# Eight float32 products of zeros ahead of TensorE's first work, in a chunked scan followed by two feed-forward layers

## The chip, the cores and the metric

One Trainium2 chip, one of its cores. The metric is the device time of one execution, in microseconds (us); lower is better. The kernel was timed in three runs; a fourth execution was recorded by the hardware profiler, and all rows below are from that one.

## The reference

Three stages, one after the other; everything is float32.

```python
# 1. chunked decayed scan, batch 4, heads 8, sequence 768, head dim 32, state 16
L = exp(cum[i] - cum[j]) * causal           # cum: running sum of log(clip(a))
y = (C B^T * L) x  +  (C state) * exp(cum)  # inside a chunk, plus the carried state
state = decay * state + sum_j B_j x_j * decay_from_j
# 2. first layer: 3072 tokens, 256 -> 2048 -> 256
h = x @ w_in;  x = where(h > 0, h, exp(min(h, 0)) - 1) @ w_out
# 3. second layer: 256 -> 1536 -> 256
g = x @ w_gate;  out = (g * sigmoid(g) * (x @ w_val)) @ w_out
```

## The kernel before, in words

The 3072 tokens are cut into 24 units of 128 tokens (unit t is chunk t // 4 of batch t % 4) and into six blocks of 512. The first layer runs block by block over 16 slices f of its width (two groups of products per slice: `h` into PSUM, L558, then `c`, L599 in block 0 and L607 in the later blocks); the second layer runs over 36 steps after it. The scan of a block's four units must be done before the block's first `h` can start. For blocks 1 to 5 that work is laid between the slices of the block before; for block 0 there is nothing in front of it, so units 0 to 3 form a prologue of about 22 us.

The order of work on each engine is the order in which the program issues it (a manual schedule; each engine takes its instructions in order). In the prologue that order is written out by hand in the string `ORDER` (L65): each word stands for one step. The words that matter here, with their lines:

- `La0`, `ca0` (L323, L329, L331): loads the decays of unit 0 as an 8-row table and clips them. `ba0` (L337) spreads that table over 128 partitions with two float32 products of 256 columns; the result is read by `E0`. `bp0`, `bp1` (L341) do the same for the running products, read by `P0`, `P1` (L355).
- `cl1` (L360, L364) clips the decays of unit 1, which came by DMA. `E0` (L350) and `E1` to `E3` (L370) are scans on VectorE over the decays. `el` (L413, ScalarE) and `bn` (L407, GpSimd) scale B with the result.
- `cb0` to `cb3` (L437): 16 small products C B^T per unit, even units into the PSUM tile `cb`, odd units into `cb_odd` (named cbo in the trace, two banks). `m0` to `m3` (L443) multiply E with them.
- `u` (L454), `sc` (L465), `sn` (L477), `y` (L524, L514), `out` (L542, ScalarE), `xl` (L546, VectorE): the unit's state, its output, and the output split into a high part `xh` and a low part `xl`, which are the operands of `h`. Units 1 and 3 share the PSUM tile yo for their outputs.
- `d00`, `d10`, `d20` and so on (L139, L142, L146, VectorE), `ex` (L136, ScalarE), `wh` (L184, ScalarE), `wl` (L190, GpSimd): decoding of float64 weights into a high and a low float32r part, `wih` and `wil`. Batch 0 (`d.0`) gives the first layer's weights of slices 0 and 1, batch 1 those of 2 and 3, batch 2 the `wov` of c in slices 0 and 1.

In block 0 a slice f goes: `m_a` (six products h, L558, into one of two PSUM buffers), `m_e1` (ScalarE, L580), `m_e1b` (ScalarE, L585, then VectorE, L586, which reads h a last time and so frees its buffer), and, two slices later, `m_c` (two float32 products c, L599). The weight decoding of the later slices is laid on VectorE between these steps.

A float32 product stands in the trace as two matmul records and two weight loads; a float32r product (L558, L607) as one of each. `zero_q` (L812) is a tile of 128x128 zeros that VectorE sets first of all; in the kernel before it is an operand of the running products at L386 alone.

Of the kernel before, what the change touches and what calls it, by code (L numbers as in the profile page):

```python
# [18 lines left out]
Q = 128  # L19
# [47 lines left out]
def ssm_mlp_glu_kernel(ctx, tc, a, bcs, xbc, w1, w2, consts, out):  # L67
    nc = tc.nc
# [10 lines left out]
    zero_q = const.tile([128, Q], F32, name="zero_q")  # L79
# [26 lines left out]
    cb_odd = first.enter_context(tc.tile_pool(name="ps0", bufs=1, space=PSUM)).tile([128, 2, 512], F32, name="cbo")  # L106
# [46 lines left out]
    def load_w1(j):  # L153
        if j >= 4:
            raw = w2e[:, j % 5 * 1024:(j % 5 + 1) * 1024]
        else:
            raw = {2: w2e[:, 1024:2048], 3: w2e[:, 5120:]}.get(j)
        kind, p = batches[j]
        w1s[j] = [None, *decode(w1.bitcast(U32)[kind == "o", p], raw)]
        w1s[j][1]()  # L160

    def ex_w1(j):
        w1s[j][2]()

    def dec_w1(j, steps=(0, 1, 2)):
        kind, p = batches[j]
        if w1s[j][0] is None:
            if kind == "i":
                w1s[j][0] = stg.tile([128, 512], F32, tag="v", name="v", bufs=VB)
            else:  # L170
                w1s[j][0] = W1["ov", p] = w1p.tile([128, 512], F32, tag="wo", name="wov", bufs=NF1 // 2)
                for i, z in enumerate(halves):
                    W1["v", 2 * p + i] = w1s[j][0][:, z]
        for k in steps:
            w1s[j][3][k](w1s[j][0])
# [5 lines left out]
    def hi_w1(j):  # L181
        kind, p = batches[j]
        if kind == "i":
            nc.scalar.activation(W1["ip", p][0], w1s[j][0], AF.Copy)  # L184

    def lo_w1(j):
        kind, p = batches[j]
        v = w1s.pop(j)[0]
        if kind == "i":
            nc.gpsimd.tensor_tensor(W1["ip", p][1], v, W1["ip", p][0].bitcast(F32), ALU.subtract)  # L190
# [620 lines left out]
    with tc.manual_schedule():  # L811
# [24 lines left out]
        for f in range(6):  # L836
            tok[f"LW{f}"] = lambda f=f: load_w1(f)
            tok[f"ex{f}"] = lambda f=f: ex_w1(f)
            for k in range(3):
                tok[f"d{k}{f}"] = lambda f=f, k=k: dec_w1(f, (k,))  # L840
            tok[f"wh{f}"] = lambda f=f: hi_w1(f)
            tok[f"wl{f}"] = lambda f=f: lo_w1(f)
        for z in ORDER:
            tok[z]()
        first.close()
# [190 lines left out]
```

## Time and profile before

| what | value |
|---|---|
| three runs | 607.23, 607.78, 607.55 us; median 607.55 |
| the profiled execution | 607.43 us |
| its span, first to last instruction | 605.6 us |
| mean granted TensorE clock | 0.998 |
| busy share | PE 98%, DVE 74%, POOL 58%, ACT 58% |

PE is TensorE's matmuls, PEld its weight loads, DVE is VectorE, ACT is ScalarE, POOL is GpSimd. The time of an execution is its span and 1.8 us around it. Matmul records overlap: the end of one is modelled and lies after the start of the next, so the rate of TensorE is read from the distance between starts, and a busy share near 100% need not be full speed. The last three columns of such a row name the operation, its tiles and their shapes; square brackets give the idle time of the engine just before, and what ended it.

### The profile page before, as it was taken

The page shows a single profiled execution, that of the slowest core. Times are in us where ns is not written, and L with a number is a line of the kernel's source. Part 1 is how long each engine was busy: PE and PEld are TensorE (multiplying, and loading weights), DVE is VectorE, ACT ScalarE, POOL GpSimd, SP SyncE. Part 2 cuts the span into 40 slices and gives each one's busy share as a digit, 9 for nine tenths or more (in the row PEclk, how much of TensorE's full clock was granted, in tenths as well). Part 3 has the DMA queues.
Part 4 walks back from the last instruction along what each step waited for, and adds up shares of the span by engine and source line. Part 5 has one row for each costly group of instructions (what it writes and reads, how often), then busy time and mean ns, then how long its engine had stood idle before and what let it go on. Part 6 is the DMA issues. An engine that isn't in the chain of part 4 may idle for free.

```text
span 605.6 us, 9763 instructions
## 1 busy us (share of the span) xinstructions
PE 593.6 (98%) x3524; PEld 469.5 (78%) x3524; DVE 450.6 (74%) x684; ACT 350.0 (58%) x623; POOL 352.4 (58%) x318
## 2 busy tenths in 40 slices
PE   5999999999999999999999999999999999999997
PEld 4656667887888888878888788887888888888785
DVE  6898867777888879985765688878766777766665
ACT  1565657776668766776976555554434444433333
POOL 3543559998888877874685667754333334333331
PEclk9999999999999999999999999999999999999999
DMA  7698533346666446732000111100100000100001
GB/s 205 251 287 239 181 99 99 129 124 172 200 200 187 176 183 202 228 127 80 27 27 26 53 53 53 52 1 1 70 1 0 1 1 1 69 1 0 2 0 69
DMA packets 22743, 58.69 MB, mean 97 GB/s; under 512 B 3736, under 2 KB 6168, under 8 KB 22696
## 3 DMA queue, kind: packets, MB, share of 16 engines
q1 hardware_dynamic: 20664, 53.18, 28.5%
q10 hardware_dynamic: 2032, 4.90, 2.1%
q8 instruction: 27, 0.44, 0.3%
q14 instruction: 20, 0.16, 0.1%
HBM read 50.12 MB, written 7.96 MB: 96 GB/s over the span
## 4 chain that ended last, share of the span: by engine, by line
PE 85%; DVE 4%; ACT 1%; issue 1%; DMA 0%; POOL 0%; SPq 0%; DVEq 0%
PE h L558 18%; PE c L607 17%; PE o L722 16%; PE pc L746 8%; PE pd L746 8%; PE pa L746 8%; PE pb L746 4%; PE cb L432 2%; PE y L509 2%; PE c L599 1%; PE y L505 1%; DVE E L370 1%; DVE m L586 0%; DVE wov L139 0%; DVE wov L142 0%
## 5 line engine op out<-in xcount | busy, mean ns | idle before, releaser
L755 POOL TENSOR_TENSOR gl<-m,gh 128x512 fp32r<-128x512 f32 x70 | 94.1, 1346 | 136.0 <-ACT gh L753 136.0
L564 POOL TENSOR_TENSOR gl<-m,gh 128x512 fp32r<-128x512 f32 x80 | 111.7, 1397 | 39.1 <-ACT gh L563 37.4
L586 DVE SCALAR_TENSOR_TENSOR m<-m,h 128x512 f32<-128x512 f32 x96 | 65.6, 683 | 50.0 <-ACT m L585 49.4
L580 ACT ACTIVATE m<-h 128x512 f32<-128x512 f32 x96 | 56.9, 593 | 48.7 <-PE h L558 43.6
L558 PE MATMUL h<-xh,wih 128*128 128x512 f32 x192 | 80.9, 423 | 0.9 <-ACT xh L542 0.6
L558 PE MATMUL h<-xh,wil 128*128 128x512 f32 x192 | 75.5, 395 | 0.0
L766 DVE TENSOR_TENSOR ident<-s,pb 128x512 f32<-128x512 f32 x36 | 24.8, 688 | 50.8 <-PE pb L746 40.2
L607 PE MATMUL c<-gh,woh 128*128 128x512 f32 x160 | 62.4, 390 | 0.0
L607 PE MATMUL c<-gh,wol 128*128 128x512 f32 x160 | 62.3, 389 | 0.0
L585 ACT ACTIVATE m<-m 128x512 f32<-128x512 f32 x96 | 59.9, 624 | 0.5
L558 PE MATMUL h<-xl,wih 128*128 128x512 f32 x192 | 60.1, 395 | 0.0
L722 PE MATMUL o<-gh,w2h 128*128 128x512 f32 x144 | 56.1, 389 | 0.0
L722 PE MATMUL o<-gh,w2l 128*128 128x512 f32 x144 | 56.0, 389 | 0.0
L722 PE MATMUL o<-gl,w2h 128*128 128x512 f32 x144 | 55.9, 389 | 0.0
L563 ACT ACTIVATE gh<-m 128x512 fp32r<-128x512 f32 x80 | 50.1, 626 | 5.9 <-DVE m L586 5.7
L783 ACT ACTIVATE pc<-pc 128x512 f32<-128x512 f32 x36 | 21.0, 582 | 53.4 <-DVE pc L781 53.4
L607 PE MATMUL c<-gl,woh 128*128 128x512 f32 x160 | 50.9, 389 | 0.0
L778 ACT ACTIVATE m<-pa 128x512 f32<-128x512 f32 x36 | 21.5, 598 | 49.4 <-PE pa L746 49.4
L392 POOL TENSOR_TENSOR xb<-xb,P 128x128 f32<-128x128 f32 x16 | 38.0, 2374 | 14.2 <-DVE P L386 14.2
L558 PEld LDWEIGHTS h<-xh,wih 128*128 128x128 f32 x192 | 36.4, 190 | 12.3 <-DVE m L586 1.5
L753 ACT ACTIVATE gh<-m 128x512 fp32r<-128x512 f32 x72 | 45.2, 628 | 0.9 <-DVE m L788 0.2
L762 ACT ACTIVATE s<-pa 128x512 f32<-128x512 f32 x36 | 21.5, 598 | 37.7 <-PE pa L746 37.7
(235 smaller groups left out, 1433.9 us busy)
## 6 DMA issues: line engine op xcount, KB each, us to landing
w2e<-in_w SPq DMA_DIRECT2D x12, 768.0 KB
abc<-ac SPq DMA_DIRECT2D x16, 512.0 KB
bcraw<-in_bcs SPq DMA_DIRECT2D x32, 256.0 KB
w2e<-in_w SPq DMA_DIRECT2D x14, 512.0 KB
xb<-in_xbc SPq DMA_DIRECT2D x18, 256.0 KB
v2d<-w2e ACTq DMA_DIRECT2D x12, 384.0 KB
v<-v2d SPq DMA_DIRECT2D x12, 384.0 KB
out_y<-x SPq DMA_DIRECT2D x12, 256.0 KB
```

The source lines that it names most:

```text
L392: nc.gpsimd.tensor_tensor(u["ct"], u["ct"], u["P"], ALU.mult)
L558: nc.tensor.matmul(dst, lhsT=l, rhs=r, start=first and i == 0, stop=last and i == len(ops) - 1, **kw)
L563: nc.scalar.activation(hi, src, AF.Copy)
L564: lo_eng.tensor_tensor(lo, src, hi.bitcast(F32), ALU.subtract)
L580: nc.scalar.activation(m, h, AF.Relu, scale=-1.0)
L585: nc.scalar.activation(m, m, AF.Exp, scale=-1.0)
L586: nc.vector.scalar_tensor_tensor(m, m, -1.0, h, ALU.add, ALU.max)
L607: nc.tensor.matmul(cps[b][m], lhsT=w[:, m * 128:(m + 1) * 128], rhs=r, start=f == 0 and w is wh and r is gh, stop=f == NF1 - 1 and r is gl)
L722: nc.tensor.matmul(ops_[p, i, m], lhsT=l, rhs=r, start=f == 0 and k == 0, stop=f == NF2 - 1 and k == 2)
L746: nc.tensor.matmul(ps[k], lhsT=l, rhs=r, start=first and i == 0, stop=i == 2, skip_group_check=True)
L753: nc.scalar.activation(hi, m, AF.Copy)
L755: eng.tensor_tensor(lo, m, hi.bitcast(F32), ALU.subtract)
```

## The change

Eight products are issued to TensorE ahead of every step of `ORDER`. Both operands are `zero_q`: 128x128 as the weights, and the same tile read four times over as 512 moving columns. They write the two banks of `cb_odd` in turn, each product as a group of its own. Nothing reads the result; `cb1` writes the same banks later, again with a start of its own.

```diff
@@ -840,6 +840,9 @@
             tok[f"wl{f}"] = lambda f=f: lo_w1(f)
+        for z in range(8):
+            nc.tensor.matmul(cb_odd[:, z % 2].rearrange("p (a q) -> p a q", q=Q), lhsT=zero_q, rhs=zero_q.unsqueeze(1).to_broadcast([128, 4, Q]),
+                             start=True, stop=True)
         for z in ORDER:
             tok[z]()
```

## Rows read from the trace of the kernel before

**Rows 1.** The page: PE's busy tenths and granted clock in 40 slices.

```profile
PE   5999999999999999999999999999999999999997
...
PEclk9999999999999999999999999999999999999999
```

**Rows 2.** Timeline of PE to 30 us: start, length, line, tiles, shape, records.

```profile
3.29 2.07 PE L337 MATMUL y<-w2e 8*128 8x256 f32 x4 [3.29 <-DVE w2e L331]
...
19.95 0.68 PE L524 MATMUL yo<-w2e,x 64*32 64x64 f32 x32
20.56 0.79 PE L514 MATMUL yo<-x,sbd 128*128 128x128 f32 x2
22.00 1.22 PE L558 MATMUL h<-xh,wih 128*128 128x512 f32 x2 [0.64 <-ACT xh L542]
23.02 1.05 PE L558 MATMUL h<-xl,wih 128*128 128x512 f32 x2
...
26.43 0.83 PE L558 MATMUL h<-xh,wil 128*128 128x512 f32 x2
27.19 0.69 PE L437 MATMUL cb<-bcraw 16*64 16x64 f32 x32
27.81 0.50 PE L558 MATMUL h<-xh,wih 128*128 128x512 f32 x1
```

**Rows 3.** Chain of work that ended last: start, length, what, number of records.

```profile
75.12 1.72 PE c L599 x4
...
95.77 1.36 PE h L558 x6
```

**Rows 4.** Line L599: durations in ns (min/median/max), first and last start, shape.

```profile
L599 PE MATMUL c<-m,wov x64: 590/592/593, 29.3 to 86.3; 128*128 128x512 f32 x64
```

**Rows 5.** Line L524: durations of one shape before and after 26 us.

```profile
L524 PE MATMUL y<-E,x x96: 216/216/241, 49.9 to 73.0; 64*32 64x64 f32 x96
...
L524 PE MATMUL yo<-E,w2e x32: 307/310/311, 17.1 to 17.7; 64*32 64x64 f32 x32
```

**Rows 6.** Timeline of DVE to 50 us.

```profile
0.83 0.17 DVE L812 MEMSET zero_q<- 128x128 f32 x1 [0.83 <-PEq L1027]
...
6.16 0.43 DVE L360 TENSOR_SCALAR abc<-abc 128x512 f32<-128x512 f32 x1 [2.73 <-DMA abc<-in_a]
...
6.70 1.27 DVE L350 TENSOR_TENSOR_SCAN E<-y,x 128x256 f32<-128x256 f32 x2
7.89 1.20 DVE L370 TENSOR_TENSOR_SCAN E<-abc,x 128x512 f32<-128x512 f32 x1
...
21.98 0.42 DVE L546 TENSOR_TENSOR xl<-yo,xh 128x256 fp32r<-128x256 f32 x1 [0.37 <-ACT xh L542]
...
26.25 0.69 DVE L586 SCALAR_TENSOR_TENSOR m<-m,h 128x512 f32<-128x512 f32 x1 [0.44 <-ACT m L585]
```

**Rows 7.** Waits of DVE, 6.7 to 26.9 us: us in total, times, longest.

```profile
DVE wov L146 <- ACT e L136: 0.6, 1, 0.6
DVE m L586 <- ACT m L585: 0.4, 1, 0.4
DVE xl L546 <- ACT xh L542: 0.4, 1, 0.4
DVE x L465 <- PE cbo L454: 0.3, 1, 0.3
DVE w2e L355 <- PE cb L341: 0.2, 1, 0.2
DVE w2e L443 <- ACT x L413: 0.2, 1, 0.2
```

**Rows 8.** Waits of PE, from 26.86 us to the end.

```profile
PE cb L432 <- DVE zc L319: 0.4, 1, 0.4
PE h L558 <- DVE m L586: 0.2, 1, 0.2
```

**Rows 9.** Waits of DVE, 24 to 90 us.

```profile
DVE x L477 <- POOL sbd L481: 4.4, 4, 1.4
```

## The prediction

> **What bounds the kernel now.** I read the page first, then TensorE's timeline, then VectorE's timeline and its waits. On the page PE is busy in every slice of the span but the first, where it is at five tenths [rows 1]: after the prologue the kernel is a queue of matmuls, and from 26.86 us to the end PE waits 0.6 us in all [rows 8]. So whatever moves the first block's products moves the end, unless something between takes it up.
>
> The prologue is the other way round. From `E0` at 6.70 us to `m0`'s last step at 26.25 [rows 6] VectorE waits six times, for 2.1 us in 20 [rows 7]; the rest is its own in-order work. PE, ScalarE and GpSimd serve it. So the question is when that run on VectorE starts, and which of its six waits go away.
>
> TensorE's clock is the third thing to see. The granted clock reads full in all 40 slices [rows 1], but the distances between starts say otherwise. Between the starts at 23.02 and 26.43 us lie eight products of 512 columns, so 0.43 us each [rows 2]; later six of the same shape take 1.36 us, 0.23 each [rows 3]. [...] The small products of line 524 show the same, 310 ns at 17 us and 216 ns from 49 us on [rows 5]. So the whole prologue ran at the low level, though PE had something in hand for much of it, and the clock rose only near 26.8 us, 4.8 us after the dense products began at 22.00.
>
> **The change part by part.**
>
> *The eight products.* A float32 product is two records; the four records of `c` in one slice take 1.72 us at the high level, 0.43 each [rows 3]. Sixteen records are 16 x 0.43 = 6.9 us at the high level and 13.8 at the low one. They wait only for `zero_q`, which VectorE has set at 0.83 + 0.17 = 1.0 us [rows 6], so I let them start at 1.05. The unknown is T, how long they run at the low level. The nearest row is the one rise in this trace, 4.8 us after dense work began. The end is then 1.05 + 6.9 + T/2 = 10.3 us. The bounds: 7.9 if the clock were high from the first record, 14.8 if it never rises under zeros. I take 10.3, as dense 512-column products are the same kind of work as that stretch; with T between 2.5 and 7, 9.2 to 11.4.
>
> [...] No row here shows a product passing another, and the sum goes by order.
>
> *What queues behind them.* `ba0` now starts at 3.29, released by VectorE's clip [rows 2], and is wanted by `E0`. `E0` starts at 6.70 because `cl1` stands ahead of it on VectorE, and that waits for a DMA until 6.16 [rows 6]. So the products are hidden only up to a point between: the second spread result is there near 5.4, 1.3 us before `E0` can use it. That cover is much shorter than the delay. New times: a record of 256 columns at the high level is half of 0.43, 0.215, and its result is there 0.16 (592 - 430 ns [rows 4]) after its columns end. The first spread, two records, is done at 10.3 + 0.59, `E0` starts about 10.95, and `E1`, 1.19 us behind it as now (7.89 - 6.70 [rows 6]), at 12.15. **VectorE's run is 4.25 us late.** `cl1`, `ca0` and the loads on the queues of SP and ACT stay where they are; nothing else was waiting.
>
> *What the higher clock gives back.* If it holds through the prologue, PE's services get shorter. Of VectorE's waits [rows 7], `P1`'s for `bp1` (0.17) and `sc3`'s for `u3` (0.29) are PE at the low level, and go: 4.25 - 0.46 = 3.8. Then `xl3` waits 0.37 for `xh3`, at the end of PE's last output, 19.95 to 21.4 us [rows 2]; that work is some 0.6 shorter at the high level, so the wait goes: 3.4. `wov`'s wait for ScalarE's `e` (0.57) stays: `e` stands behind a weight step that itself waits for VectorE. `m0`'s wait (0.44) is for exp after relu after the first `h`. Those six `h` take about 2.6 us at the low level and 1.4 at the high one, so `h` is done before ScalarE is free, and this wait goes: 3.4 - 0.44 = **2.95 us**. The fifth, on `el3` (0.17), is ScalarE's own and stays.
>
> *TensorE itself.* The last `h` stretch, 22.00 to about 27.2 for twelve products [rows 2], is 2.4 us shorter at the high level (12 x 0.2). `h0` would start near 25.2, `h1` end near 28.4. But the slice-2 product, at 27.81 now, needs the PSUM buffer that `m0` frees, near 29.8. PE is 2.0 us late there, VectorE 2.95.
>
> *What is late next.* In block 0 VectorE goes on with weight decoding between the `m` steps. Its only waits there are four for GpSimd's `sbd`, 4.4 us [rows 9], a round trip that VectorE itself starts and that is late with it. So its 2.95 is passed on from step to step, while PE, 2.0 late, has some 0.9 more to lose: near 73.5 us PE waits 0.2 for an `m` already [rows 8], so at that place there is no room between the two. From there PE is the bound and carries 2.95 to the end. The DMA loads behind the prologue are issued 3 to 4 us later, as their buffers are; each is wanted by VectorE about as much later.
>
> *The sum.* 4.25 - 0.17 - 0.29 - 0.37 - 0.44 = +2.95 us (rounding within 0.05). The profiled execution took 607.43 us (span 605.6 and 1.8 around it), 0.12 under the median of 607.55, so it stands for the runs. Forecast: 607.55 + 2.95 = **610.5 us**. In short the shift is the end of the zeros less 7.35 us; 9.2 to 11.4 gives +1.85 to +4.05, 609.4 to 611.6.
>
> **The rivals.**
>
> *The clock falls again before `h`.* The zeros raise it, but between 11 and 25 us PE does the same broken small work that did not raise it before, with stops behind VectorE. Then only `P1`'s 0.17 is given back, with T as above +4.1 us: 611.6 (610.5 to 612.7). For it: the low level through all of the prologue [rows 5]. Against: no row shows a fall. [...] Chance 0.18.
>
> *The zeros do not raise the clock*, so the change does not do what a warm-up would. They end at 14.8, the spreads run at the low level (four records in 1.87 us, from 3.29), `E1` starts near 17.5, 9.6 late, and almost nothing comes back: 617 us. Against: the column work is as dense as that which raised it at 22 us. Chance 0.06.
>
> *Not slower: the clock rises at once.* One rise in one trace does not fix when the next one comes. The place is the first two zero records, the price T/2; it decides at T = 1.2 us, where the zeros end at 8.55 and the shift is 1.2, 608.75 us. At T = 0 it is 7.9 - 7.35 = +0.6, 608.1. All six waits of VectorE taken off [rows 7] would bring that to 4.25 - 2.1 - 2.4 = -0.2, so a gain that can be told from nothing is almost out of reach. Against: the dense products from 22 us on kept the low level for about eleven in a row. Chance 0.10, with some room for a shift that is taken up by VectorE's waits for `sbd`.
>
> **How the numbers follow.** The forecast has 0.63, the three rivals 0.18, 0.06 and 0.10; 0.03 is left for a gain by a way I do not see. The range takes the forecast's own bounds, a few tenths for VectorE steps that change length as they fall beside others, and most of the falling clock: 608.9 to 612.4. The 617 case and most of the not-slower case are left out. About 0.2%, 1.2 us, is what a measurement of this kernel can tell from no change. Slower by more: 0.63 + 0.18 + 0.06 = 0.87; within: 0.10; faster: 0.03.
>
> **What would show it.** Sixteen records from about 1.05 us, the first 0.85 apart and the later 0.43; the last result near 10.3. `E0` starting near 11, released by PE and not by VectorE's order. Line 524 at 216 ns and the first `h` at 0.23 apart, near 25.2 us; 310 ns or 0.43 there would mean that the clock fell. `m0` near 29.2 instead of 26.25. PE waits for `m` a few times between 30 and 73 us, and from 75 us on the same rows, all later by one amount. Wrong would be: zeros done by 8.5, VectorE idle less than 3 us ahead of `E0`, or a lag at 30 us that has gone by 75.

## The result, and the profile after

The changed kernel is **slower: 611.62 us median of four runs (610.60 to 613.60), against 607.66 us for the kernel before (its three runs and one more). The ratio is 1.0064, 95% interval 1.0051 to 1.0077**, that is 3.96 us. Timed again it took 611.87 us (611.46 to 612.38) against 607.61, ratio 1.0070 (1.0057 to 1.0083). The forecast was 610.5 in a range of 608.9 to 612.4.

The profiled execution took 610.60 us, the shortest of the four, with a span of 608.8, 3.2 more than before. Its page has these lines in the place of [rows 1]; the slices are 15 us long:

```profile
PE   7899999999999999999999999999999999999997
...
PEclk9699999999999999999999999999999999999999
```

The granted clock now shows a fall, in the second slice. Its timeline of TensorE (start, length, line, tiles, shape, records, and in brackets the idle time before), to set beside [rows 2]:

```profile
1.05 8.53 PE L844 MATMUL cbo<-zero_q 128*128 128x512 f32 x16 [1.05 <-DVE zero_q L812]
9.51 1.12 PE L337 MATMUL y<-w2e 8*128 8x256 f32 x4
...
13.37 0.35 PE L454 MATMUL y<-xb 64*32 64x64 f32 x16 [1.43 <-POOL xb L407]
14.09 0.80 PE L341 MATMUL cb<-w2e 8*128 8x130 f32 x2 [0.37 <-DVE w2e L355]
...
23.66 0.85 PE L524 MATMUL yo<-w2e,x 64*32 64x64 f32 x32
24.44 0.49 PE L514 MATMUL yo<-x,sbd 128*128 128x128 f32 x2
25.68 0.73 PE L558 MATMUL h<-xh,wih 128*128 128x512 f32 x2 [0.75 <-ACT xh L542]
26.25 0.63 PE L558 MATMUL h<-xl,wih 128*128 128x512 f32 x2
...
28.66 0.69 PE L437 MATMUL cb<-bcraw 16*64 16x64 f32 x32
30.20 0.50 PE L558 MATMUL h<-xh,wih 128*128 128x512 f32 x1 [0.85 <-DVE abc L364]
```

The zeros hold TensorE from 1.05 to 9.51, 8.46 us; at the high level alone they would need 6.88, so by the sum's own rule they ran (8.46 - 6.88) x 2 = 3.2 us at the low level. Behind them stands the spread, L337, which started at 3.29 before. The first `h` products, 0.23 apart, are at the high level. In between the clock had been down: the table of stretches of this execution gives, after the busy times of the five engines, the granted clock, the DMA share and GB/s:

```profile
9.51:14.10 4.59, 2.79 (x88) 2.24 (x87) 3.36 (x6) 0.43 (x2) 0.98 (x1) 1.00 0.83 264
14.10:24.40 10.30, 8.83 (x248) 6.63 (x248) 9.17 (x25) 2.38 (x7) 7.09 (x15) 0.50 0.63 204
24.40:31.00 6.60, 5.00 (x51) 3.63 (x50) 5.71 (x13) 4.92 (x10) 3.09 (x3) 1.00 0.53 183
```

Where 0.50 is granted, the records of L524 that start from 20.9 to 21.4 us take 311 ns (median), as the 310 of the low level in [rows 5]. VectorE's timeline, to set beside [rows 6]:

```profile
6.29 0.43 DVE L360 TENSOR_SCALAR abc<-abc 128x512 f32<-128x512 f32 x1 [2.79 <-DMA abc<-in_a]
...
10.74 1.27 DVE L350 TENSOR_TENSOR_SCAN E<-y,x 128x256 f32<-128x256 f32 x2 [3.88 <-PE y L337]
11.93 1.20 DVE L370 TENSOR_TENSOR_SCAN E<-abc,x 128x512 f32<-128x512 f32 x1
...
14.93 0.43 DVE L355 TENSOR_TENSOR_SCAN w2e<-cb,x 128x130 f32<-128x130 f32 x1 [0.18 <-PE cb L341]
...
21.23 0.28 DVE L477 SCALAR_TENSOR_TENSOR x<-x,w2e,y 128x64 f32<-128x64 f32 x1 [0.55 <-ACT xh L542]
...
25.66 0.42 DVE L546 TENSOR_TENSOR xl<-yo,xh 128x256 fp32r<-128x256 f32 x1 [0.35 <-ACT xh L542]
...
29.47 0.68 DVE L586 SCALAR_TENSOR_TENSOR m<-m,h 128x512 f32<-128x512 f32 x1
...
75.92 0.67 DVE L586 SCALAR_TENSOR_TENSOR m<-m,h 128x512 f32<-128x512 f32 x1
```

The last of these `m` stood here in the kernel before:

```profile
72.74 0.67 DVE L586 SCALAR_TENSOR_TENSOR m<-m,h 128x512 f32<-128x512 f32 x1
```

`E0` has a new wait, 3.88 us for the spread, and starts 4.04 late. At `xl3` it is 3.68, at the first `m` 3.22 (its wait for ScalarE is gone), and at the `m` of 75.92 us 3.18. The span grew by 3.2. So from the first `m` on the lateness goes through block 0 whole, and TensorE now waits there more than in [rows 8] (the first line is its wait for the first `m`, put down to a small VectorE step that ends beside it):

```profile
PE h L558 <- DVE abc L364: 0.8, 1, 0.8
...
PE h L558 <- DVE m L586: 0.7, 2, 0.4
PE cb L432 <- DVE zc L319: 0.5, 1, 0.5
```

### The profile page after: what moved, and what is told of

Same layout as the page of the kernel before. It is cut to its first block, busy times and chain, and to the rows that moved or that the text cites. A ratio compares the mean times of both kernels' runs of the same rounds, so it can differ in the third digit from the quotient of the medians.

```text
span 608.8 us, 9795 instructions
## 1 busy us (share of the span) xinstructions
PE 597.1 (98%) x3540; PEld 468.9 (77%) x3540; DVE 450.2 (74%) x684; ACT 349.9 (57%) x623; POOL 353.5 (58%) x318
## 4 chain that ended last, share of the span: by engine, by line
PE 84%; DVE 3%; ACT 1%; issue 1%; POOL 0%; DVEq 0%; ACTq 0%
PE h L558 18%; PE c L607 17%; PE o L722 16%; PE pd L746 8%; PE pc L746 8%; PE pa L746 8%; PE pb L746 4%; PE cb L432 2%; PE y L509 2%; PE c L599 1%; PE y L505 1%; DVE E L370 1%; DVE wov L142 0%; DVE zc L319 0%; DVE m L586 0%
```

## The experiments

Two theories stood after this. A: the time is the lateness of VectorE's run behind products that stand ahead of it in TensorE's order. B: what the clock does after the zeros decides what is left of it, and makes the spread of 3 us between runs. Each experiment is set against the kernel before, timed beside it (medians of 607.55 to 607.61 us).

**The changed kernel once more.** No edit.

> The changed kernel once more, unaltered, for the spread of its time. Theory A (place in the order): the eight products push E0 back by about 4.0 us and everything behind it on VectorE with it; the first profiled run lost 3.2 us that way. Theory B (clock): how long TensorE stays at the low level after its fall near 14 us differs from run to run, and that is the spread of 610.6 to 613.6: runs whose mean granted clock is 0.991 come out near 610.6, runs at 0.985 or less at 611.5 and above. If B is wrong, time and mean clock do not go together.

Five runs: 611.46 to 612.38, at mean clocks of 0.985 to 0.989, so none at 0.991 and none near 610.6, as B has it; among themselves they show no order by clock (611.87 at 0.989, 611.46 at 0.985). That neither shows B nor rules it out. The execution of 613.60 us, at 0.985 too, has no trace, and why it took 2 us longer stays open; the kernel before has such executions as well (609.87 beside a median of 607.61). The trace of the 611.87 us execution, span 610.1:

```profile
10.58 1.13 PE L337 MATMUL y<-w2e 8*128 8x256 f32 x4
...
26.69 1.22 PE L558 MATMUL h<-xh,wih 128*128 128x512 f32 x2 [0.47 <-ACT xh L542]
27.70 1.05 PE L558 MATMUL h<-xl,wih 128*128 128x512 f32 x2
28.56 1.05 PE L558 MATMUL h<-xh,wil 128*128 128x512 f32 x2
29.41 0.88 PE L558 MATMUL h<-xh,wih 128*128 128x512 f32 x2
```

Two things differ from the first one, and both cost. The clock rose later (starts 0.85 apart up to 5.48 us and not 3.77), so the zeros ended at 10.58 and not 9.51. And it was still down at the first `h`, 0.43 apart up to 29 us:

```profile
16.35:26.69 10.34, 8.61 (x249) 6.34 (x249) 9.28 (x25) 3.70 (x9) 6.39 (x14) 0.50 0.45 158
26.69:29.03 2.34, 2.34 (x6) 1.86 (x7) 1.78 (x4) 1.21 (x2) 1.05 (x2) 0.50 0.45 137
```

```profile
11.81 1.27 DVE L350 TENSOR_TENSOR_SCAN E<-y,x 128x256 f32<-128x256 f32 x2 [4.72 <-PE y L337]
...
30.95 0.69 DVE L586 SCALAR_TENSOR_TENSOR m<-m,h 128x512 f32<-128x512 f32 x1 [0.61 <-ACT m L585]
```

`E0` started at 11.81, 5.11 late, and the first `m` at 30.95, 4.70 late, with its wait of 0.6 us for ScalarE kept. So the two executions of one kernel differ by 1.07 us in where the zeros end, and by 0.41 in what comes back on the way to `m` (0.82 against 0.41).

**Three products.**

```diff
-        for z in range(8):
+        for z in range(3):
```

> Three products of zeros in place of eight. Six records: four at 0.85 and two at 0.43 end near 5.3 us, the first spread is read near 6.5, and E0 starts at 6.70 as in the kernel before. Theory A: no difference to the kernel before beyond 0.5 us either way. Theory B, or a cost that lies in the products' mere presence: 1 us or more slower than before, as the clock rises at 4.5 us and falls again in the prologue all the same.

607.81 us against 607.61, ratio 1.0002 (0.9992 to 1.0013): no difference that can be told, as A has it. In the profiled execution the clock stayed low for all six records (0.85 apart up to the last, at 5.47 us), and the spread came later than expected:

```profile
6.47 1.13 PE L337 MATMUL y<-w2e 8*128 8x256 f32 x4
```

```profile
7.70 1.27 DVE L350 TENSOR_TENSOR_SCAN E<-y,x 128x256 f32<-128x256 f32 x2 [0.75 <-PE y L337]
...
73.72 0.67 DVE L586 SCALAR_TENSOR_TENSOR m<-m,h 128x512 f32<-128x512 f32 x1
```

`E0` began at 7.70, 1.0 late, and the `m` of 73.72 us is still 0.98 late. That execution took 608.21, 0.4 above the median; how late `E0` was in the other eleven is not known. The clock rose all the same (the 32 records of `cb0` at 7.75 us took 0.69, against 1.13 in the kernel before) and fell again near 10 (granted 1.00 up to 9 us, 0.92 from 9 to 10, 0.50 behind that), so a rise and a fall by themselves cost nothing that the median shows.

**Sixteen products.**

```diff
-        for z in range(8):
+        for z in range(16):
```

> Sixteen products of zeros. 32 records, four of them at 0.85 and 28 at 0.43, end near 16.5 us; E0 would start near 17.7, 11 us later than in the kernel before. Theory A: 9.5 to 10.5 us slower than before, that is 0.86 us for each product beyond the eighth. Rival: the first block has slack behind the prologue that takes up more of a longer delay, or the cost is the clock's: under 6 us slower.

618.60 against 607.61, 11.0 us slower (ratio 1.0180, 1.0167 to 1.0194): A, and a little above its range, because the zeros ended at 18.04 and not 16.5.

```profile
18.04 1.13 PE L337 MATMUL y<-w2e 8*128 8x256 f32 x4
```

```profile
19.28 1.27 DVE L350 TENSOR_TENSOR_SCAN E<-y,x 128x256 f32<-128x256 f32 x2 [12.49 <-PE y L337]
...
38.34 0.69 DVE L586 SCALAR_TENSOR_TENSOR m<-m,h 128x512 f32<-128x512 f32 x1 [0.54 <-ACT m L585]
...
84.81 0.67 DVE L586 SCALAR_TENSOR_TENSOR m<-m,h 128x512 f32<-128x512 f32 x1
```

`E0` is 12.58 late, the first `m` 12.09, the `m` of 84.81 us 12.07. There is no slack behind the prologue that takes up more of a longer delay.

**VectorE held back instead, without zeros.**

```diff
+        def wait_ve():
+            for _ in range(4):
+                nc.vector.memset(ident8, 0.0)
+        tok["dv"] = wait_ve
...
-... bp0 cl1 E0 el0 ...
+... bp0 cl1 dv E0 el0 ...
```

> No zeros on TensorE; instead VectorE sets a tile of 1024 columns to zero four times just ahead of E0 (about 3.6 us in all, by the length of its small memsets; the tile is written again before it is read). TensorE's work and clock stay as in the kernel before. Theory A: E0 and everything behind it late by that time, and the kernel slower by the same, 3.2 to 4.0 us, since no wait is given back. Rival: the lateness of VectorE is taken up in block 0 and it is TensorE's own delay that counted: under 1.5 us slower.

611.29 against 607.61, 3.68 us slower (ratio 1.0060, 1.0047 to 1.0073). The memsets took longer than estimated (0.91 us each, 1.19 from start to start), so `E0` was 4.58 late; the first `m` was 3.88 late.

```profile
11.28 1.21 DVE L350 TENSOR_TENSOR_SCAN E<-y,x 128x256 f32<-128x256 f32 x2
...
30.13 0.69 DVE L586 SCALAR_TENSOR_TENSOR m<-m,h 128x512 f32<-128x512 f32 x1 [0.38 <-ACT m L585]
...
76.57 0.67 DVE L586 SCALAR_TENSOR_TENSOR m<-m,h 128x512 f32<-128x512 f32 x1
```

That is nearly the loss of the change, with no zeros and TensorE's clock low through the prologue as before (the first `h` records 0.43 apart from 26.89 to 29.45 us). The lateness of VectorE's run is enough to explain the time. It also says that the 0.7 us that came back here owe nothing to the clock: three VectorE steps that stood between 11 and 18 us before came 0.15 us closer to the ones ahead of them, and `sc3`'s wait of 0.3 shrank to 0.2.

**The eight products behind `cb1`.** They write the tile of the odd units' outputs before its first use.

```diff
-        for z in range(8):
-            nc.tensor.matmul(cb_odd[:, z % 2] ...
...
+        def fill():
+            for k in range(8):
+                nc.tensor.matmul(y_odd[:, k % 2] ...
...
+        tok["fz"] = fill
...
-... E1 el1 cb1 Labc3 ...
+... E1 el1 cb1 fz Labc3 ...
```

> The eight products moved behind cb1, into the tile of the odd units' outputs, so that they start near 7.7 us, after the spreads. E0, E1 and m0 then run on time (E0 at 6.70). Theory A (what counts is who queues behind them on TensorE): now u0 waits, which sc0 on VectorE reads at 10.50, and bp1, which P1 reads: with the end of the zeros near 7.7 + 6.9 + 2.4 = 17, u0 is there near 17.5, VectorE stands still for about 6.5 us, and the kernel is 6 to 7.5 us slower. Rival: only the spread of E0 matters, and the kernel loses less than 2 us.

614.61 against 607.55, 7.06 us slower (ratio 1.0120, 1.0106 to 1.0134). `E0` was on time, at 6.72, and the stop moved to the reader of `u0`:

```profile
6.72 1.27 DVE L350 TENSOR_TENSOR_SCAN E<-y,x 128x256 f32<-128x256 f32 x2
...
17.31 0.23 DVE L465 COPY x<-y 128x64 f32<-128x64 f32 x1 [6.70 <-PE y L454]
```

So it is not the spread that is dear, but whatever of VectorE's order stands behind the zeros.

**Two more products in TensorE's stops.**

```diff
+        def fill():
+            for k in range(1):
+                nc.tensor.matmul(y_odd[:, k % 2] ...
...
+        tok["fz"] = fill
...
-... E1 el1 cb1 Labc3 ...
+... E1 el1 cb1 fz Labc3 ...
...
-... u0 bp1 m1 sc0 ...
+... u0 bp1 fz m1 sc0 ...
```

> The changed kernel with two more products of zeros, one after cb1 and one after bp1, where TensorE stood idle for 1.4 and 0.5 us just ahead of the clock's fall at 14.4 us; they write the tile of the odd units' outputs before its first use. Theory: the stops let the clock fall, so here it stays high past 14.4 us, at least to 16.5. If it then holds to the first h, the waits of P1 (0.2), of sc3 and sn1 (0.3 to 0.5), of xl3 (0.35) and of m0 (0.4 to 0.6) are short and the kernel is 2.7 to 3.2 us slower than the kernel before instead of 4; if it falls a little later, it is as slow as the changed kernel, 3.8 to 4.3. Rival: the products add work and no gain, 4.5 us or more.

612.03 against 607.55, 4.5 us slower (ratio 1.0080, 1.0066 to 1.0093): nothing gained. (In the first trace of the changed kernel the clock fell near 14.1 us and not at 14.4, so the stop behind `bp1` came after the fall.) The theory behind it fell too. TensorE had no stop from 1.05 us on (12.65 us busy in 12.65), and the clock fell in the middle of the first added product all the same:

```profile
1.05:13.70 12.65, 12.65 (x87) 6.43 (x88) 2.87 (x8) 2.13 (x3) 0.60 (x4) 0.99 0.78 207
13.70:27.44 13.74, 12.67 (x270) 7.53 (x268) 12.06 (x31) 3.84 (x10) 8.22 (x17) 0.50 0.50 178
```

What TensorE did just ahead of the fall was the 32 small products of `cb0` and `cb1` (64 records), one behind the other; the added product of `cb1` took 1.92 us for its two records, against 1.13 in the next run, where the granted clock was 1.00 at that place.

```profile
12.63 0.65 PE L437 MATMUL cbo<-x 16*64 16x64 f32 x32
13.21 1.92 PE L848 MATMUL yo<-zero_q 128*128 128x512 f32 x2
```

**Three products and the two in the stops.** Both edits above.

> Three products at the start and the same two more in TensorE's stops: the clock rises near 6 us at the price of at most 1 us on E0 (7.70 against 6.70 in the trace of three products). If the high clock can be kept to the first h, it gives back 0.8 to 1.3 us of VectorE's waits, and the kernel is equal to the kernel before or up to 0.5 us faster. If it falls in the prologue all the same: 0 to 1 us slower, as three products alone (0.2).

608.28 against 607.55, ratio 1.0009 (1.0000 to 1.0018): 0.7 us slower, at the edge of what can be told. The clock fell near 10.5 us (granted 0.73 from 10 to 11 us, 0.50 behind that), and no gain was left.

**`E0` ahead of `cl1`, without zeros.** If lateness is passed on whole, earliness might be too, and this version could beat the kernel before.

```diff
-... bp0 cl1 E0 el0 ...
+... bp0 E0 cl1 el0 ...
```

> The kernel before, without zeros, with E0 put ahead of cl1 on VectorE: E0 then does not stand behind the DMA that cl1 waits for, and can start when both spreads are there, near 5.5 us instead of 6.70, and E1 near 7.2 instead of 7.89. If lateness of VectorE's run is passed on one for one, earliness should be too, up to 0.7 us, so far as the loads that the prologue waits for (unit 2's B and C near 11.5 us) allow: 0.2 to 0.6 us faster, which is at the edge of what can be measured. Rival: the prologue's end is set by those loads or by TensorE, and nothing comes of it: within 0.2 us.

607.66 against 607.59, ratio 1.0000 (0.9991 to 1.0009): nothing. `E0` started at 5.64, 1.06 early, but GpSimd's `bn2` waits for a load in both kernels and started only 0.09 us earlier; it also took longer. The kernel before, then this one:

```profile
14.16 0.40 POOL L407 TENSOR_TENSOR x<-x 128x128 f32<-128x128 f32 x1 [0.47 <-DMA x<-in_xbc]
```

```profile
14.07 1.02 POOL L407 TENSOR_TENSOR x<-x 128x128 f32<-128x128 f32 x1 [0.96 <-DMA x<-in_xbc]
```

In the kernel before that load held up GpSimd alone; now it is on VectorE's path, as the products behind `bn2` and the output that `sn0` waits for (17.29 here) are late in turn:

```profile
5.64 1.27 DVE L350 TENSOR_TENSOR_SCAN E<-y,x 128x256 f32<-128x256 f32 x2 [2.04 <-PE y L337]
...
17.29 0.28 DVE L477 SCALAR_TENSOR_TENSOR x<-x,w2e,y 128x64 f32<-128x64 f32 x1 [1.11 <-ACT xh L542]
...
21.72 0.42 DVE L546 TENSOR_TENSOR xl<-yo,xh 128x256 fp32r<-128x256 f32 x1 [0.34 <-ACT xh L542]
...
72.47 0.67 DVE L586 SCALAR_TENSOR_TENSOR m<-m,h 128x512 f32<-128x512 f32 x1
```

At `xl3` 0.26 us of the 1.06 were left, and at the `m` of 72.47 us 0.27: what comes out of the prologue early is passed on, but it is less than the medians can show. No version tried beats the kernel before.

## Why the prediction was right or wrong

**Right: the direction, the size within its range, and the place.** The zeros push `E0` back, VectorE's in-order run carries it, the block behind passes it on whole. The experiment on VectorE alone and the one with sixteen products show each half of that by itself. The median is 1.1 us above the forecast, 1.4 when timed again, and lies within the range because the range took in most of the rival of the falling clock. That the first trace lost 3.2 us, so near to 2.95, is luck: the zeros ended 0.8 us earlier than the sum has it, `E0` stood 0.6 further behind them, and 0.5 less came back.

**The end of the zeros.** Taken as 10.3 us with bounds of 9.2 to 11.4: 9.51 and 10.58 in the two traces of this kernel, 10.84 in the one with two more products. The time at the low level varies from run to run, 3.2 us here, 6.5 us by the same rule with sixteen products ((18.04 - 1.05 - 13.76) x 2), and with it most of the spread between the executions traced. The starts of the records say the same: they go from 0.85 to 0.43 us apart behind about 3.8 us in the first trace, 5.5 in the second and 7.2 with sixteen. They also show the factor of two that T/2 takes between the levels; of the rows, [rows 2] and [rows 3] give 0.43 to 0.23, and none has float32 records of 512 columns at the low level.

**`E0` behind the spread: mis-sized.** The step let `E0` start 0.65 us after the zeros, when the first of the two spread products is done. It starts 1.23 after (9.51 to 10.74, 10.58 to 11.81, 18.04 to 19.28): one wait (3.88 us in the first trace) covers both products. In the first trace that was hidden by the earlier end of the zeros: 4.04 late, 4.25 forecast. In the second it was not, 5.11.

**What the higher clock gives back: the step that failed.** It assumed that the clock holds through the prologue, and took 1.3 us off. It fell at about 14 us in the first trace and 16 in the second (granted 0.50 from 14.10 to 24.40, and from 16.35 to 29.03 at least), and came back before the first `h` in one and after it began in the other. Of the four waits counted off, `P1`'s was still 0.18 in the first trace and gone in the second, where the step behind it took 0.66 us instead of 0.40; `xl3`'s was still 0.35 and 0.55; `sc3`'s shrinks with no help from the clock; only `m`'s 0.44 went as reasoned, in the one trace where the first `h` ran at the high level. `sn0` had a new wait of 0.55 in the first trace, for `xh`, which the sum does not have. So 0.8 us came back in one and 0.4 in the other, and the rest of the 0.8 is in the main the closer steps of VectorE that the run without zeros shows as well.

**The rival that the clock falls again**, given 0.18, is what happened in both traces of this kernel, and its 611.6 us is nearer to the medians of 611.62 and 611.87 than the forecast's 610.5. Its reason is not shown. The first trace has stops of 1.43 and 0.37 us ahead of the fall, but does not show that they caused it; in the run with two more products the clock fell with no stop at all (12.65 us busy in 12.65). Nor did small work always leave the clock low: in the first trace it rose again near 24.4 us, in the middle of the small products of L524 and L514 (granted 0.50 up to there, 1.00 behind). What makes it fall and rise within the prologue stays open.

**The other rivals.** The clock does rise under the zeros (starts 0.85 us apart, then 0.43; 0.06 for not), and it does not rise at once: three products at the low level ran 5.4 us before the spread. The cover of 1.3 us was rightly read: ahead of `cl1`, `E0` started at 5.64. In the kernel before the spread's records end at 5.36 (3.29 + 2.07), and with the 0.11 that `E0` stands behind them in the first trace (9.51 + 1.12 to 10.74) it could by estimate have started at 5.47, 1.2 us ahead of its 6.70. The spread stayed behind the zeros, as the sum has it (all 16 records ahead of it at 9.51 and 10.58, all 32 at 18.04). Among small products the order was not strict, though: the trace of the kernel before has one record of L524 (`y1`) at 17.07 us, ahead of seven of L454 (`u3`), issued earlier, that start from 17.12 on.

**The carry to the end.** Slice 2's first product was foreseen near 29.8 us and came at 30.20; the `m` before TensorE's wait near 73 us was 3.18 late and the span 3.2 longer. The other traces agree: the first `m` and the `m` near 73 us are 0.98 and 0.98 late with three products, 3.88 and 3.83 with VectorE held back, 12.09 and 12.07 with sixteen. Passed on whole, as argued.

## What to carry to other kernels

Products put ahead to raise a clock stand in the engine's order like any others (here the spread started at 9.51 and 10.58 us and not at 3.29); ask first which engine's run begins behind them, and how much cover the first reader has. Here it was 1.3 us, and the eight products took 8.5 to 9.8. A clock raised before a stretch of small, broken products need not be there at the end of it (here it fell at about 14 and 16 us, ahead of the first `h` at 25.68 and 26.69), so count nothing back that rests on its holding. And a run that passes lateness on whole need not pass on as much earliness: a load that only another engine had waited for can come onto its path, as it did for `bn2`.

## What was not expected of the hardware

The clock fell with TensorE continuously busy, after 32 small products (64 records) in about 1.1 us (the run with two more products, near 13.4 us: granted 1.00 from 12 to 13 us, 0.70 from 13 to 14, 0.50 behind that). And the granted clock reads 1.00 from the first microsecond on in the traces of the kernel before, of the changed kernel (both) and of three products, over stretches whose starts show the low level (records 0.85 apart from 2.92 to 5.47 us with three products); a fall after the first rise it does show, as 0.50. So a mean clock of 0.998, as the kernel before had, says nothing of a start at half speed, and the changed kernel's 0.985 to 0.991 does not mean that more of it ran slow.
